# Fetching w1's first piece later and its rest in one transfer, in a kernel of block-sorted attention and routed experts

## The chip, the cores and the metric

The kernel runs on one core of a Trainium2 chip. The core has five engines that work side by side, each with its own queue of instructions: TensorE (PE in the profile, matmuls; PEld its weight loads), VectorE (DVE), ScalarE (ACT), GpSimd (POOL) and SyncE (SP, which here only issues transfers). Sixteen DMA engines move data between the chip's memory and the core's. The metric is the device time of the whole kernel in microseconds (us).

## The reference: what is computed

```python
P = sort_net                                  # 4 x 8 heads, 8 x 8
for _ in range(5):
    P = exp(P - max(P)); P = P / sum(P, rows); P = P / sum(P, columns)
k_sorted = einsum('bhij,bhjcd->bhicd', P, k_blocks)     # 8 blocks of 96 rows
v_sorted = einsum('bhij,bhjcd->bhicd', P, v_blocks)
attn = softmax(scale * q_blocks @ k_sorted.T)           # inside each block
x = (attn @ v_sorted), laid out as 3072 x 512
P = exp(x @ w_gate - max), balanced 8 times over rows and columns
for e in range(8):
    out += P[:, e:e+1] * (maximum(x @ w1[e], 0) @ w2[e])
```

The attention has 4 batches of 8 heads, 768 positions and 64 columns; w1 is 8 x 512 x 1024 and w2 is 8 x 1024 x 512. All inputs are float32 in memory; the kernel works in bfloat16 from the load on.

## The kernel before

The kernel has two stages. In the first, the attention of the four batches is worked out batch by batch, and expert 0 of a batch is computed beside it (lines 97 to 487). In the second (from line 488), experts 1 to 7 follow for all tokens, with seven products of half-size blocks in place of eight. The change lies at the start of the first stage, in the first 30 us.

**Loads.** Whatever has to become bfloat16 on its way is loaded by GpSimd (`load_batch`, `load_rest`, `part_w1`, `load_w2`), and stands in GpSimd's one queue in the order in which it is written. For batch 0 these are the queries, values and keys in halves of four heads (lines 98 and 100), then the first 256 of the 1024 columns of expert 0's w1 (line 108). `part_w1(f0, f1)` (lines 103 to 106) loads such a strip of columns as one transfer: 128 partitions times 4 rows of f1 - f0 columns.

**Sort matrices.** VectorE and ScalarE work out P (lines 426 to 445); TensorE spreads it over the partitions into `pbps` (line 452). `Rt[bb]` is the sorting matrix of a batch, one 128x128 matrix per head. For batch 0 VectorE builds it (line 456); for batch 1 GpSimd does, with the generator `build_r(1, nc.gpsimd, 4)`: two instructions of four heads each (line 133), each followed by a `yield`, so that the caller can put something between them. They read `Pb`, which ScalarE copies at line 464.

**The values' exchange.** `sort_values(0, ...)` multiplies the values by the sort matrices (line 146) and evicts them to `vs` (line 148). The sorted rows then have to move to other partitions: eight transfers of 96 KB, one for each block i (lines 154 to 161), take them from `vs` to `vsb`. For batch 0 their order is 0, 1, 2, 3, 4, 6, 5, 7. Blocks 1 and 3 are issued by ScalarE, 5 and 7 by GpSimd, the others by SP; before block 5 the generator yields, so 5 and 7 are issued only when `values` is resumed at line 467. A transfer that ScalarE or GpSimd issues takes its place among that engine's own instructions.

**The plan.** What TensorE does next is written out by hand in `PLAN0` (line 209), and `pin` keeps each engine's instructions in the order of the program. A letter is a kind of work and its digits are heads and halves: k keys, s scores, d sums, m the mix of scores and values (line 261, the first reader of `vsb`), w warming matmuls whose result nobody reads (line 423), e and h a block of 128 columns of expert 0's hidden layer, l the logits. The steps e00 to e11 (`begin`, line 358) compute hidden blocks 0 and 1, from w1's columns 0 to 255; each h1 (`expert_hidden`, line 368) computes the next block, from 2 (columns 256 to 383) up to 7:

```python
PLAN0 = ("k0 k1 w2 s00 k2 s10 k3 w1 s20 D00 d10 w2 s30 d20 w4 d30 m00 s01 m10 m20 m30 w1 e00 e10 "
         "s11 d01 e01 e11 s21 d11 m01 h1 s31 d21 m11 h1 h1 d31 m21 h1 h1 m31 h1 l0 l3")
```

After the exchange, GpSimd issues the rest of w1 in two pieces (lines 468 and 469), then batch 1's values, half of its keys and queries, expert 0's w2, and the other halves (lines 470 to 472).

Of the kernel before, what the change touches and what calls it, by code (L numbers as in the profile page):

```python
# [20 lines left out]
def mkap(t, dims, off=0):  # L21
    return bass.AP(tensor=t.tensor, offset=t.offset + off, ap=dims)
# [3 lines left out]
def kernel(  # L26
# [11 lines left out]
    nc = tc.nc  # L38
# [33 lines left out]
    def load_batch(bb, parts):  # L72
        for d, name in ((vt, "vt"), (kt, "kt"), (qt, "qt")):
            d[bb] = kvp.tile([128, 8, 384], BF16, name=name, bufs=2)
        load_rest(bb, parts)

    def load_rest(bb, parts):
        for x, l0, n in parts:
            d, src = {"v": (vt, v), "k": (kt, k), "q": (qt, q)}[x]
            pin(nc.gpsimd.dma_start(  # L80
                out=d[bb][:, l0:l0 + n, :],
                in_=src[bb, l0:l0 + n].rearrange("h (p kk) d -> p h (kk d)", kk=6)))
# [9 lines left out]
    def load_w2(e):  # L92
        w2t[e] = (wq if e else wcp).tile([128, 8, Dm], BF16, name="w2e")
        pin(nc.gpsimd.dma_start(out=w2t[e],
                                in_=moe_w2[e].rearrange("(fb k) f -> k fb f", k=128)))
# [7 lines left out]
    def part_w1(f0, f1):  # L103
        pin(nc.gpsimd.dma_start(
            out=w1t[0][:, :, f0:f1],
            in_=moe_w1[0, :, f0:f1].rearrange("(kk k) f -> k kk f", k=128)))

    part_w1(0, 256)
    wg = ones.tile([128, 4, E], BF16)
    pin(nc.gpsimd.tensor_copy(wg, wgf))  # L110
    mask16 = ones.tile([128, 16], F32)
# [17 lines left out]
    def build_r(bb, eng, n):  # L129

        Rt[bb] = perp.tile([128, 8, 8, 16], BF16, name=f"R{bb % 2}")
        for h in range(0, 8, n):
            ins = eng.tensor_tensor(
                out=mkap(Rt[bb], [Rt[bb].ap[0], [16, 8 * n], [1, 16]], off=h * 128),
                in0=mkap(Pb, [Pb.ap[0], [1, 8 * n], [0, 16]], off=(bb * 8 + h) * 8),
                in1=mkap(mask16, [mask16.ap[0], [0, 8 * n], [1, 16]]),
                op=ALU.mult)
            if eng is nc.gpsimd:
                pin(ins)
            yield  # L140


    def sort_values(bb, bank, n=8, h0=0):
        for h in range(h0, n):
            vps = bank([128, 384], F32)
            pin(nc.tensor.matmul(vps, Rt[bb][:, h].rearrange("p i c -> p (i c)"),  # L146
                                 vt[bb][:, h, :], start=True, stop=True))
            (nc.vector.tensor_copy if bb == 0 and h in (3, 5, 7) or bb and h % 2 else
             nc.scalar.copy)(
                vs[:, :, h, :], vps.rearrange("p (kk d) -> p kk d", d=64))  # L150
            if h % 2:
                yield

        for i in (0, 1, 2, 3, 4, 6, 5, 7) if bb == 0 else range(NB if n == 8 else 0):
            eng = ((nc.scalar if i in (1, 3) else nc.gpsimd if i in (5, 7) else nc.sync)
                   if bb == 0 else nc.gpsimd if i % 2 and bb == 1 else nc.sync)
            if bb == 0 and i == 5:
                yield
            (pin if bb == 0 else lambda ins: ins)(eng.dma_start(
                out=mkap(vsbt[bb % 2], [[VW, 96], [1, 512]], off=i * 512),  # L160
                in_=vs[16 * i:16 * i + 16].rearrange("p kk h d -> p kk (h d)")))
# [3 lines left out]
    def queries(bb, hp, bank):  # L165

        qps = bank([128, 6, 128], BF16)
        if bb < 2:

            for kk in range(6):  # L170
                for h in range(2):
                    pin(nc.tensor.matmul(qps[64 * h:64 * h + 64, kk, :],
                                         qt[bb][:, 2 * hp + h, kk * 64:kk * 64 + 64],
                                         Ibig, is_transpose=True, start=True, stop=True))
        else:
            qr = sp.tile([128, 6, 2, 64], BF16, name="qr", bufs=2)
            nc.gpsimd.tensor_copy(
                qr.rearrange("p kk h d -> p h kk d"),
                qt[bb][:, 2 * hp:2 * hp + 2].rearrange("p h (kk d) -> p h kk d", d=64))
            for kk in range(6):  # L180
                pin(nc.tensor.matmul(qps[:, kk, :], qr[:, kk].rearrange("p h d -> p (h d)"),  # L181
                                     Ibig, is_transpose=True, start=True, stop=True))
        qT[bb, hp] = sp.tile([128, 128, 6], BF16, name="qTs", bufs=4)
        (pin if bb == 0 else lambda ins: ins)(
            (nc.scalar.copy if bb == 0 or hp < 2 or bb == 1 else nc.vector.tensor_copy)(
                qT[bb, hp], qps.rearrange("p kk c -> p c kk")))
# [126 lines left out]
    def attention(bb, bank, fill):  # L313

        def sorts():
            for b in {1: (1, 2), 2: (3,), 3: ()}[bb]:
                yield from sort_values(b, bank)
                yield
# [95 lines left out]
    with tc.tile_pool(name="ps0", bufs=7, space=bass.MemoryType.PSUM,  # L414
                      reuse_waits="tile") as ps0, \
            tc.tile_pool(name="psw", bufs=1, space=bass.MemoryType.PSUM) as psw:
        bank0 = lambda shape, dt: ps0.tile(shape, dt, name="bank", tag="bank")
        unread = psw.tile([128, 4, 128], F32)

        def warm(n):  # L420

            for _ in range(n):
                pin(nc.tensor.matmul(unread, Ibig, mkap(Ibig, [Ibig.ap[0], [0, 4], [1, 128]]),
                                     start=True, stop=True))

        pin(nc.vector.reduce_max(out=rs, in_=P, axis=AX.X))
        pin(nc.vector.tensor_sub(P, P, mkap(rs, [rs.ap[0], rs.ap[1], [0, 8]])))
        for it in range(5):
            pin(nc.scalar.activation(out=P, in_=P, func=AF.Exp))
            if it >= 2:  # L430
                queries(0, it - 2, bank0)
            if it == 3:
                warm(4)
            pin(nc.vector.reduce_sum(out=rs, in_=P, axis=AX.X))
            pin(nc.vector.reciprocal(out=rs, in_=rs))
            pin(nc.vector.tensor_mul(P, P, mkap(rs, [rs.ap[0], rs.ap[1], [0, 8]])))
            pin(nc.vector.reduce_sum(out=cs, in_=Pt, axis=AX.X))
            if it == 0:
                pin(nc.vector.tensor_scalar_add(cs, cs, 1e-9))
            pin(nc.vector.reciprocal(out=cs, in_=cs))  # L440
            pin(nc.vector.tensor_mul(Pr.rearrange("p i j -> p j i") if it == 4 else Pt, Pt,
                                     mkap(cs, [cs.ap[0], cs.ap[1], [0, 8]])))
        for eng, i0, n in ((nc.vector.tensor_copy, 0, 5), (nc.scalar.copy, 5, 3)):
            pin(eng(Prep[:, i0:i0 + n],
                    mkap(Pr, [Pr.ap[0], [8, n], [1, 8], [0, 16]], off=i0 * 8)))
        pin(nc.vector.reduce_sum(out=mask16, in_=Ibig.rearrange("p (j c) -> p c j", c=16),
                                 axis=AX.X))
        queries(0, 3, bank0)
        warm(3)
        pbps = bank0([128, 8, 32], F32)  # L450
        for i in range(8):
            pin(nc.tensor.matmul(pbps[:, i, :], Prep[:, i].rearrange("p j c -> p (j c)"),
                                 Ibig[0:32, 0:32], start=True, stop=True))
        Rt[0] = perp.tile([128, 8, 8, 16], BF16, name="R0")
        for h in range(0, 8, 2):
            nc.vector.tensor_tensor(
                out=Rt[0][:, h:h + 2],
                in0=mkap(pbps, [pbps.ap[0], [1, 2], [32, 8], [0, 16]], off=h),
                in1=mkap(mask16, [mask16.ap[0], [0, 2], [0, 8], [1, 16]]), op=ALU.mult)
        warm(2)  # L460
        values = sort_values(0, bank0)
        for _ in range(5):
            next(values)
        nc.scalar.copy(Pb, pbps.rearrange("p i g -> p g i"))
        for _ in build_r(1, nc.gpsimd, 4):
            pass
        next(values, 0)
        part_w1(256, 512)
        part_w1(512, 1024)
        load_batch(1, [("v", 0, 8), ("k", 0, 4), ("q", 0, 4)])  # L470
        load_w2(0)
        load_rest(1, [("k", 4, 4), ("q", 4, 4)])
        def tiles():
            yield from expert_hidden(0, begun["h"], lambda: bank0([128, 512], F32))

        first_attention(bank0, warm, tiles())
# [335 lines left out]
    for m, o in enumerate(ends):  # L812
        e, p, hT, _ = chunks[-1]
# [4 lines left out]
    for r in range(len(pairs) + 6):  # L818
        n, i = r // 4, r % 4
# [84 lines left out]
```

## Time and profile before

| | |
|---|---|
| time, median of 3 runs | 665.8 us (665.04 to 665.95) |
| the profiled execution | 665.01 us, span 663.2 us |
| TensorE busy | 650.9 us, 98% of the span |
| GpSimd busy | 465.9 us, 70% |
| VectorE busy | 475.5 us, 72% |
| ScalarE busy | 386.3 us, 58% |
| TensorE's clock | 0.999 of full speed in the mean |
| transfers issued by GpSimd | 26.81 MB, 25.8% of the 16 DMA engines' time |
| TensorE busy from 0 to 50 us | 41.68 us |
| TensorE busy from 50 to 650 us | 599.8 us |

The span runs from the first to the last instruction of the profiled execution; the device time is a little longer. Every time below counts from the span's start. A group of instructions is named by line, engine, operation and what it writes and reads, with its count, its busy time, the mean duration, and the idle time of the engine just before it with the cause of that. A transfer has two times: when the engine issues it, and how long after that its last byte has landed.

### The profile page before, as it was taken

Reading aid. Unit: us, or ns where it says so; the run is one execution under the profiler, and the core shown is the slowest. Engines: PE = TensorE matmul, PEld = TensorE weight load, DVE = VectorE, ACT = ScalarE, POOL = GpSimd, SP = SyncE. Lnnn points to the kernel's source line nnn. Section 1 sums busy time; section 2 is a strip of 40 time slices with the busy share of each in tenths; the row PEclk is TensorE's granted clock in tenths of the full one; section 3 lists DMA queues with packets and bytes.
Section 4 is the critical chain, followed back from the end, with each engine's and each line's share of the span. In section 5 each row is a group of like instructions: output and inputs, shape, how many; then the busy total and the mean of one; then the engine's idle time right before and its main releaser. Section 6 shows DMA issues by size and latency. Waiting matters only on the chain.

```text
span 663.2 us, 13141 instructions
## 1 busy us (share of the span) xinstructions
PE 650.9 (98%) x5047; PEld 422.3 (64%) x5047; DVE 475.5 (72%) x910; ACT 386.3 (58%) x757; POOL 465.9 (70%) x430
## 2 busy tenths in 40 slices
PE   5999999999999999999999999999999999999997
PEld 2555565555666666666666666666666666666665
DVE  6856576666777777777777777777777777777775
ACT  5777657476777755555555555555555655555540
POOL 3543540196999898779796979698797969846641
PEclk9999999999999999999999999999999999999999
DMA  9999944004303040120303040302103040000224
GB/s 151 177 223 142 195 73 65 1 1 73 55 1 64 1 65 1 27 38 3 61 1 65 1 64 2 65 1 40 26 0 64 1 65 2 1 1 33 96 80 175
DMA packets 33743, 36.52 MB, mean 55 GB/s; under 512 B 2064, under 2 KB 27088, under 8 KB 33680
## 3 DMA queue, kind: packets, MB, share of 16 engines
q0 software_dynamic: 26448, 26.81, 25.8%
q1 hardware_dynamic: 6720, 8.29, 4.4%
q8 instruction: 39, 0.64, 0.4%
q10 hardware_dynamic: 512, 0.59, 0.3%
q14 instruction: 24, 0.20, 0.1%
HBM read 52.45 MB, written 6.29 MB: 89 GB/s over the span
## 4 chain that ended last, share of the span: by engine, by line
PE 96%; DMA 2%; DVE 1%; POOL 1%; issue 0%; ACT 0%; POOLq 0%
PE bk L601 38%; PE oacc L712 38%; PE bank L381 5%; PE bank L368 5%; DMA kt<-in_k_dram 2%; PE bank L220 1%; PE bank L261 1%; PE oacc L784 1%; PE bk L678 1%; PE bank L243 1%; PE bank L196 1%; PE bk L776 1%; PE bank L146 1%; PE oacc L776 1%; PE bk L784 1%; PE bank L181 0%
## 5 line engine op out<-in xcount | busy, mean ns | idle before, releaser
L662 DVE SCALAR_TENSOR_TENSOR osbl<-oacc,glog,osbl 128x256 f32<-128x256 f32 (+1 forms) x411 | 219.4, 535 | 125.6 <-PE oacc L712 116.3
L587 ACT ACTIVATE hT<-bk 128x512 bf16<-128x512 f32 (+1 forms) x176 | 104.2, 592 | 147.5 <-PE bk L601 130.7
L601 PE MATMUL bk<-xtT,w1e 128*128 128x512 bf16 x504 | 149.1, 379 | 0.0
L712 PEld LDWEIGHTS <-hs 128*128 128x128 bf16 x984 | 96.3, 98 | 62.9 <-issue 0.3
L712 PEld LDWEIGHTS <-hT 128*128 128x128 bf16 x904 | 88.4, 98 | 57.9 <-issue 0.6
L702 POOL TENSOR_TENSOR hs<-hT 128x512 bf16<-128x512 bf16 x82 | 95.1, 1159 | 39.8 <-DVE hT L590 34.3
L712 PE MATMUL oacc<-w2e,hT 128*128 128x256 bf16 x764 | 114.6, 273 | 0.2
L702 POOL TENSOR_TENSOR hs<-hs,hT 128x512 bf16<-128x512 bf16 x82 | 94.7, 1154 | 6.4
L601 PE MATMUL bk<-xc,wc 128*128 128x512 bf16 x336 | 99.1, 379 | 0.1
L702 POOL TENSOR_TENSOR hs<-hT,hs 128x512 bf16<-128x512 bf16 x82 | 94.6, 1153 | 6.4
L712 PE MATMUL oacc<-w2e,hs 128*128 128x256 bf16 x616 | 92.4, 273 | 0.0
L601 PEld LDWEIGHTS <-w1e 128*128 128x128 bf16 x672 | 65.8, 98 | 11.6 <-issue 0.3
L590 DVE CUSTOM_DVE_ANT_0 hT<-bk,p 128x512 bf16<-128x512 f32 x84 | 58.1, 691 | 7.7 <-PE bk L601 3.1
L636 ACT COPY p<-bk 128x512 f32<-128x512 f32 x84 | 49.1, 585 | 24.3 <-PE bk L601 23.4
L630 ACT COPY u<-bk 128x512 f32<-128x512 f32 x84 | 49.2, 585 | 22.2 <-PE bk L601 22.1
L621 ACT COPY bk<-bk 128x512 f32<-128x512 f32 x84 | 48.0, 572 | 20.5 <-PE bk L601 20.5
L590 DVE CUSTOM_DVE_ANT_0 hT<-bk,u 128x512 bf16<-128x512 f32 x84 | 57.1, 680 | 1.1 <-PE bk L601 0.6
L712 PE MATMUL oacc<-w2s,hs 128*128 128x256 bf16 x368 | 55.2, 273 | 0.0
L601 PEld LDWEIGHTS <-wc 128*128 128x128 bf16 x504 | 49.3, 98 | 8.0 <-issue 0.2
L655 DVE SCALAR_TENSOR_TENSOR s<-bk,hT 128x512 bf16<-128x512 f32 x80 | 54.4, 680 | 0.0
L601 PE MATMUL bk<-xc,w1e 128*128 128x512 bf16 x168 | 50.0, 379 | 0.0
L601 PE MATMUL bk<-xtT,wc 128*128 128x512 bf16 x168 | 50.0, 379 | 0.0
(140 smaller groups left out, 828.9 us busy)
## 6 DMA issues: line engine op xcount, KB each, us to landing
w2e<-in_moe_w_dram POOLq DMA_DIRECT2D x8, 1024.0 KB, 9.5
w1e<-in_moe_w_dram POOLq DMA_DIRECT2D x7, 1024.0 KB, 8.1
out_dram<-osbl SPq DMA_DIRECT2D x21, 256.0 KB, 2.0
vsb<-vs SPq DMA_DIRECT2D x24, 96.0 KB, 3.1
vt<-in_v_dram POOLq DMA_DIRECT2D x3, 768.0 KB, 11.8
qt<-in_q_dram POOLq DMA_DIRECT2D x4, 384.0 KB, 10.5
kt<-in_k_dram POOLq DMA_DIRECT2D x4, 384.0 KB, 12.2
kt<-in_k_dram POOLq DMA_DIRECT2D x2, 768.0 KB, 15.0
```

The costliest lines, as they stand in the source:

```text
L368: pin(nc.tensor.matmul(hps[:, 0:n], w1t[0][:, kk, fb * 128:(fb + 1) * 128], xtT[:, kk, c0:c0 + n], start=(kk == 0), stop=(kk == 3)))
L381: pin(nc.tensor.matmul(oacc, hTs[:, fb, tt * 128:(tt + 1) * 128], w2t[0][:, fb, :], start=(fb == 0), stop=(fb == 7)))
L587: relu = lambda o, x: nc.scalar.activation(out=o, in_=x, func=AF.Relu)
L590: return nc.vector._custom_dve(TENSOR_ADD_SAT, out=o, in0=x, in1=y, s0=TOP, s1=0.0)
L601: pin(nc.tensor.matmul(ps, wa[:, kk, :], xa[:, kk, :], start=(first and kk == 0), stop=(kk == 1), skip_group_check=True))
L621: pin(nc.scalar.copy(t["w"], t["u"]))
L630: pin(nc.scalar.copy(t["u2"], t["u"]))
L636: pin(nc.scalar.copy(t["p5"], t["v"]))
L655: pin(nc.vector.scalar_tensor_tensor(out=s3[:, i, :], in0=t["w"], scalar=0.0, in1=c12, op0=ALU.max, op1=ALU.subtract))
L662: pin(nc.vector.scalar_tensor_tensor(out=o, in0=ps, scalar=glog[:, t, e:e + 1], in1=o, op0=ALU.mult, op1=ALU.add))
L702: pin(nc.gpsimd.tensor_tensor(out=s[:, c], in0=a, in1=b, op=o))
L712: pin(nc.tensor.matmul(ps, h[:, fb, :], w[:, fb, :], start=(first and fb == 0), stop=(fb == 3), skip_group_check=True))
```

## The change

It has three parts. The load of w1's first 256 columns is taken from its place behind batch 0's loads and is put between the two instructions with which GpSimd builds batch 1's sort matrices. The rest of w1, so far two transfers of 256 and 512 columns, becomes one of 768 columns at the place of the two. And block 3 of batch 0's exchange is issued by SP, not by ScalarE, which keeps block 1.

```diff
@@ -105,7 +105,6 @@
-    part_w1(0, 256)
     wg = ones.tile([128, 4, E], BF16)
     pin(nc.gpsimd.tensor_copy(wg, wgf))
@@ -152,7 +151,7 @@
         for i in (0, 1, 2, 3, 4, 6, 5, 7) if bb == 0 else range(NB if n == 8 else 0):
-            eng = ((nc.scalar if i in (1, 3) else nc.gpsimd if i in (5, 7) else nc.sync)
+            eng = ((nc.scalar if i == 1 else nc.gpsimd if i in (5, 7) else nc.sync)
                    if bb == 0 else nc.gpsimd if i % 2 and bb == 1 else nc.sync)
@@ -462,11 +461,12 @@
         nc.scalar.copy(Pb, pbps.rearrange("p i g -> p g i"))
-        for _ in build_r(1, nc.gpsimd, 4):
-            pass
+        half = build_r(1, nc.gpsimd, 4)
+        next(half)
+        part_w1(0, 256)
+        next(half, 0)
         next(values, 0)
-        part_w1(256, 512)
-        part_w1(512, 1024)
+        part_w1(256, 1024)
         load_batch(1, [("v", 0, 8), ("k", 0, 4), ("q", 0, 4)])
```

## The prediction

> **What bounds the kernel now.** I read the page's first two parts, then the chain of waits from 0 to 80 us, then TensorE's groups in the stretch the change touches, then GpSimd's and ScalarE's timelines there and the DMA issues one by one. TensorE is busy 98% of the span. The chain of waits (start us, length us, what) says where the rest sits:
>
> ```profile
> 5.69 11.89 DMA kt<-in_k_dram
> 17.58 0.04 issue
> 17.62 0.53 PE bank L196 x12
> ...
> 24.01 0.71 PE bank L358 x4
> ...
> 26.66 0.17 PE bank L261 x8
> 26.83 0.76 PE bank L368 x4
> ```
>
> Until 17.58 the chain is the load of the keys; from there it is TensorE without a break, the warming matmuls of L423 included. TensorE's groups between 17.6 and 33 us (busy, mean ns, then idle before and its cause) say the same:
>
> ```profile
> L368 PE MATMUL bank<-xtT,w1e 128*128 128x384 bf16 x24 | 4.6, 328 | 0.0
> L261 PE MATMUL bank<-atp,vsb 96*64 96x96 bf16 x48 | 2.0, 207 | 0.0
> L358 PE MATMUL bank<-xtT,w1e 128*128 128x384 bf16 x8 | 1.7, 326 | 0.0
> L196 PE MATMUL bank<-R,kt 128*64 128x128 bf16 x24 | 1.1, 222 | 0.2 <-DMA kt<-in_k_dram 0.2
> ```
>
> The values' exchange (vsb, read at L261) and all of w1 (L358, L368) arrive in time; only the last keys are 0.2 us late. So nothing of TensorE's can be saved here but that 0.2 us (0.6 with the 0.39 us idle at 15.73, whose cause is ScalarE's eviction of L148), and whatever makes TensorE wait is paid in full, because its order is written out by hand and it is full up to the last microseconds.
>
> GpSimd, whose queue carries every load that casts (start, length):
>
> ```profile
> 6.42 0.79 POOL L104 DMA_DIRECT2D w1e<-in_moe_w_dram  x1
> ...
> 16.47 2.07 POOL L133 TENSOR_TENSOR R<-Pb,mask 128x512 bf16<-128x512 f32 x2 [9.05 <-ACT Pb L464]
> 18.49 1.12 POOL L159 DMA_DIRECT2D vsb<-vs  x2
> 19.58 1.59 POOL L104 DMA_DIRECT2D w1e<-in_moe_w_dram  x2
> 21.13 0.93 POOL L80 DMA_DIRECT2D vt<-in_v_dram  x1
> ```
>
> The DMA issues around 20 us, with the time from issue to landing in the last column, for w1's second and third piece (issued at 19.58 and 20.41):
>
> ```profile
> w1e<-in_moe_w_dram POOLq DMA_DIRECT2D x1, 256.0 KB, 6.6
> w1e<-in_moe_w_dram POOLq DMA_DIRECT2D x1, 512.0 KB, 8.4
> ```
>
> and, from the page, for the whole w1 tiles loaded later on:
>
> ```profile
> w1e<-in_moe_w_dram POOLq DMA_DIRECT2D x7, 1024.0 KB, 8.1
> ```
>
> The reader should set landings against first uses. First piece: 6.42 + 12.5 = 18.9, used at 24.01, 5.1 us to spare. Second: 19.58 + 6.6 = 26.2, used (hidden block 2, columns 256 to 383) at 26.83, 0.6 us to spare. Third: 20.41 + 8.4 = 28.8, used (block 4) after blocks 2 and 3, about 29.0, 0.2 us to spare. These two margins are what the change touches.
>
> **The change, part by part.**
>
> *w1's first piece leaves the early queue.* It was the last of the early loads, behind the keys; its packets (512 B) run from 15.5 to 18.6 us in the trace's packet records, mostly after the keys' own. The keys may land up to 0.2 us earlier (their whole lateness), or not at all.
>
> *It is issued between GpSimd's two sort matrices.* The first matrix ends at 16.47 + 1.05 = 17.52. The issue takes 0.79, so 17.52 to 18.3; the second matrix runs 18.3 to 19.35 (not read before 33.31, L146); the two exchange blocks are issued at 19.35 and 19.9 instead of 18.49 and 19.06; the rest of w1 at about 20.45 to 21.25, and the next batch's values at 21.2 instead of 21.13, since one issue was added ahead and one removed. The exchange blocks 5 and 7 landed 3.7 us after issue, so 23.1 and 23.6, or two more if they queue behind the piece; L261 needs them at 26.49. Covered. The piece itself: exchange block 5, issued by GpSimd at 18.49, had its first packet at 20.1, 1.6 us later, so the piece's packets start near 19.1; 512 rows on 16 engines are 32 rows of 60 ns each, 1.9 us; with the spread between the engines seen at the first queries (2.5 us of packets, 3.8 us from first packet to landing, so 1.3) it lands near 22.3, up to 1 us later beside the other exchange transfers. Needed at 24.01. By the row of the second piece (6.6 us) it would be 24.1. So 0 to 0.3 us of wait, most likely none.
>
> *One exchange block from ScalarE's queue to SP's.* ScalarE's two issues take 16.36 to 17.88, and its first exponential starts at 17.93, though its scores were ready about 17.45:
>
> ```profile
> 16.36 1.52 ACTq L159 DMA_DIRECT2D vsb<-vs  x2
> 17.93 2.21 ACT L234 ACTIVATE atp<-bank 96x384 bf16<-96x384 f32 x5 [1.05 <-DVE kTs L202]
> ```
>
> ScalarE gains up to 0.5 us and TensorE nothing, as it doesn't wait for it. On SP, block 3 takes the third place (17.56), and blocks 4 and 6 slip by 0.6 to 0.9 us. Block 3 lands at 17.56 + 4.1 = 21.7 instead of 17.09 + 4.3 = 21.4; L261 reads it at about 22.5. Blocks 4 and 6 land by 24, read from 26.49. With w1's piece out of the way until 19.1 they should land sooner than that. Cost zero; 0.8 us would have to be lost before TensorE saw it.
>
> *w1's rest in one piece.* This is the term that counts. Hidden block 2 needed a piece of 256 KB; it now needs the last byte of 768 KB. When does that land? Start from the old third piece, 28.8, the moment at which all of w1 was there. Three things move it. (a) The first piece is now in the same stretch of queue ahead of it: 32 rows x 60 ns = +1.9 us. (b) The queue, which had a pause, starts again at 17.52 rather than 18.49: -1.0. (c) One piece has 1536-byte rows instead of 512 and 1024: by the packet records 60, 79, 98 and 172 ns for 512, 768, 1024 and 2048 bytes, so about 136 for 1536, and 32 x (60 + 98) = 5.1 us become 32 x 136 = 4.4: -0.7. Sum +0.2: it lands at 29.0. Block 2 then starts 0.04 later (the keys' landing to L196, above) instead of at 26.83: **29.04 - 26.83 = 2.2 us of wait**. Everything queued behind it on TensorE (the other hidden blocks, the mixes, batch 1) moves by as much. Of what comes after, the next values land at 32.6 and are read at 33.31, now 35.5, and the later loads have the same gain in margin, so no second wait follows. What was gained or lost before block 2, within 2 us, is swallowed by this wait: the keys' 0.2, ScalarE's 0.5, a late first piece.
>
> Bounds of that landing, both from rows. Early: a whole w1 tile with a quiet queue, 8.1 us for 1 MB, of which 32 x 172 ns = 5.5 are its rows; with 4.4 in their place 7.0, so 27.4, a wait of 0.6. Late: the whole tile issued at 64.22 beside an exchange, 10.5 us: 30.9, a wait of 4.1. I take 29.0, nearest to the 8.4 of the piece issued at the same place beside the same neighbours.
>
> On the merging, the row first: the second and third piece landed 2.6 us apart, with 3.1 us of rows in the third, so no fixed cost stood between them that a merge could remove. [...]
>
> **The sum.** 0 (exchange) + 0 (first piece) + 2.2 (rest of w1) with nothing given back. The profiled execution took 665.01 us around a span of 663.2; so 667.2. The three runs have a median of 665.8, 0.8 above it, so **668.0** for a median.
>
> **The rivals.**
>
> 1. *No wait: one transfer beats two and lands before 26.8.* Then all that is left is the keys' 0.2 us, at most 0.6: 665.2 to 665.6, not slower. It decides at 6.4 us from issue to landing. For it: 512 rows instead of 1024, and an exchange that is out of the way earlier. Against: no load of w1 without anything else in the queue was below 8.1 in the median, and the 256 KB piece took 6.6. [...] Chance 7%.
> 2. *A short wait.* The landing is between 26.8 and 28.1, towards the early bound, because the exchange on SP's queue is done sooner: 0.1 to 1.3 us, 665.9 to 667.1. Chance 19%.
> 3. *The wait slows TensorE's clock.* The first four warming matmuls at 7.87, after 6.4 idle us, took 1.89 us; four at 21.13 took 1.04. About 3.4 us after 6.44 ran at half speed, which is 1.7 us lost. If a gap of 2.2 us does the same: 668.0 + 1.7 = 669.7. Against: after the 1.11 us gap before L452 the two warming matmuls at 13.14 took 0.60, full speed; a gap of 2.2 is between the two. [...] Chance 8%.
> 4. *A later landing*, 30 to 31 us, wait 3.2 to 4.2: 669.0 to 670.0. Chance 8%.
>
> My forecast, landing between 28.1 and 30.0, is 667.1 to 669.0, chance 58%. The measurement tells about 0.2% (1.3 us) from no change; so slower 58 + 8 + 8 = 74%, same 23% (rival 2 and most of rival 1), faster 3%, for a saving that no row explains. The range 666.0 to 669.7 leaves out rival 1, a little of rival 2 and the upper part of 3 and 4.
>
> **What would show it.** Right: L368's first matmul at about 29 us with some 2 us of idle time before it, put down to the DMA of w1e; the rest of w1 issued near 20.4 and landing 8 to 9 us later; L358 and L261 without idle time; ScalarE's first exponential near 17.5; warming matmuls of later stretches unchanged. Wrong: L368 without idle time, or idle time before L358 or L261 that is longer than that before L368, or matmuls of 128x384 that take twice their 326 ns after the gap.

## The result, and the profile after

The changed kernel takes 669.79 us (median of 7 runs, 667.52 to 671.56), the kernel before 665.47 us (median of 7, 664.99 to 665.95). The ratio is 1.0062, 95% interval [1.0042, 1.0081]: 4.3 us slower, where 2.2 was forecast, and 0.1 us above the top of the stated range. The profiled execution took 670.72 us (span 668.9), 5.7 more than that of before. From the removed line 108 to the change at line 465, line numbers are one lower than before (L368 is now L367, L261 is L260, L358 is L357).

TensorE's groups between 17.6 and 36 us of the changed kernel:

```profile
L367 PE MATMUL bank<-xtT,w1e 128*128 128x384 bf16 x13 | 3.6, 415 | 3.2 <-DMA w1e<-in_moe_w_dram 3.2
L260 PE MATMUL bank<-atp,vsb 96*64 96x96 bf16 x48 | 2.4, 221 | 0.9 <-DMA vsb<-vs 0.9
L357 PE MATMUL bank<-xtT,w1e 128*128 128x384 bf16 x8 | 1.7, 326 | 0.0
L195 PE MATMUL bank<-R,kt 128*64 128x128 bf16 x24 | 1.1, 223 | 0.2 <-DMA kt<-in_k_dram 0.2
```

Two idle times are new: 0.9 us ahead of the first mix, which waits for an exchange block, and 3.2 us ahead of hidden block 2, which waits for w1. A third sign stands in the mean of L367, 415 ns where it was 328. The keys' 0.2 is still there. GpSimd, and the DMA issues at 17.6 and 20.8 us with their time to landing:

```profile
17.47 0.82 POOL L104 DMA_DIRECT2D w1e<-in_moe_w_dram  x1
18.30 1.07 POOL L132 TENSOR_TENSOR R<-Pb,mask 128x512 bf16<-128x512 f32 x1
19.31 1.11 POOL L158 DMA_DIRECT2D vsb<-vs  x2
20.40 0.82 POOL L104 DMA_DIRECT2D w1e<-in_moe_w_dram  x1
```

```profile
w1e<-in_moe_w_dram POOLq DMA_DIRECT2D x1, 256.0 KB, 7.0
vsb<-vs SPq DMA_DIRECT2D x1, 96.0 KB, 6.0
...
w1e<-in_moe_w_dram POOLq DMA_DIRECT2D x1, 768.0 KB, 10.6
```

The first piece lands at 17.47 + 7.0 = 24.5, block 3 (issued by SP at 17.55) at 23.55, the rest of w1 at 20.40 + 10.6 = 31.0. The chain of waits, from the sort matrices on:

```profile
18.30 1.07 POOL R L132
19.37 1.03 POOL vsb L158 x2
20.40 10.58 DMA w1e<-in_moe_w_dram
31.03 1.46 PE bank L367 x4
```

GpSimd's queue and one transfer now are the chain, and hidden block 2 starts at 31.03 instead of 26.83: 4.2 us. Its four matmuls take 1.46 instead of 0.76. Why, the stages show (length, busy time of PE with its count, and of PEld, DVE, ACT and POOL, then TensorE's granted clock, the DMA engines' share and GB/s):

```profile
27.50:30.90 3.40, 0.37 (x10) 0.20 (x6) 0.90 (x2) 2.06 (x5) 0.00 (x0) 1.00 1.23 187
30.90:34.30 3.40, 3.27 (x24) 1.63 (x25) 0.99 (x2) 1.26 (x4) 0.00 (x0) 0.50 1.32 202
34.30:40.00 5.70, 5.63 (x68) 3.45 (x67) 4.57 (x10) 2.00 (x4) 0.00 (x0) 1.00 1.27 205
```

After the wait TensorE's clock is granted at half for 3.4 us. Batch 1's first values (L145) start at 39.02 instead of 33.31, 5.7 us later: 4.2 of wait and 1.5 of slow clock. The 0.9 us at the exchange are inside the 4.2, not on top: without them TensorE would only have waited longer at block 2.

The clock also orders the runs. The two with a mean of 1.000 took 667.52 and 667.86 us; the four at 0.996 and 0.997 (in the profiled one, 0.997, one half-speed stretch of 3.4 us) 668.76 to 670.72; the one at 0.994 (no profile; by its size two stretches) 671.56.

### The profile page after: what moved, and what is told of

It is laid out like the page before. It is cut to its first block, busy times and chain, and to the rows that moved or that the text cites. A ratio compares the mean times of both kernels' runs of the same rounds, so it can differ in the third digit from the quotient of the medians.

```text
span 668.9 us, 13140 instructions
## 1 busy us (share of the span) xinstructions
PE 652.4 (98%) x5047; PEld 422.8 (63%) x5047; DVE 475.6 (71%) x910; ACT 386.9 (58%) x757; POOL 465.8 (70%) x429
## 4 chain that ended last, share of the span: by engine, by line
PE 94%; DVE 2%; DMA 2%; ACT 1%; POOL 1%; issue 0%
PE bk L601 38%; PE oacc L712 37%; PE bank L380 5%; PE bank L367 5%; DMA w1e<-in_moe_w_dram 2%; PE oacc L784 1%; PE bk L678 1%; PE bank L219 1%; PE bank L260 1%; PE bk L776 1%; PE bank L242 1%; PE bank L195 1%; PE bank L145 1%; PE oacc L776 1%; PE bk L784 1%; PE bank L180 0%
```

## The experiments

The theory after the result: hidden block 2 needs one part in six of the merged transfer but has to wait for its last byte, and a wait of that length costs the clock on top. The rivals: the first piece's later place does it, by pushing everything behind it back; or block 3's place on SP's queue; or the transfer is late because it is one large one. Each time is the median of its runs, beside runs of the kernel before on the same chip.

**The rest of w1 in one piece, alone** (`merge_only`; before with)

```diff
-        part_w1(256, 512)
-        part_w1(512, 1024)
+        part_w1(256, 1024)
```

> The kernel before with w1's rest in one transfer of 768 columns, nothing else: the first piece stays in the early queue and block 3 on ScalarE's queue. Theory 1 (the forecast's: what counts is when the last byte of w1 lands, and merging by itself makes that earlier): the rest lands about 0.7 us sooner than the old third piece, at 28.1, and TensorE waits 1.3 us before hidden block 2 at full clock: 666.8 us, +1.3. Rival (the rows of the merged piece are slow beside what shares the queue, whoever is ahead of it): it lands near 31 as in the changed kernel, a wait of 3 to 4 us and half the clock for 3.4 us: +4 to +6 us. Rival that the first piece's place alone is what costs: no wait, 665.5.

Measured: 669.4 us against 665.54, ratio 1.0053 [1.0041, 1.0066]: +3.9. The rest lands at 19.74 + 9.8 = 29.5, and the group of block 2 shows

```profile
L368 PE MATMUL bank<-xtT,w1e 128*128 128x384 bf16 x20 | 5.7, 445 | 3.0 <-DMA w1e<-in_moe_w_dram 3.0
```

This one edit brings 3.9 of the 4.3 us. Theory 1 as I had sized it (28.1, +1.3) is wrong: merging did not make the end of w1 earlier, but 0.6 us later (GpSimd ran 0.16 late in this execution; 29.4 against 28.8). The rival had the kind of loss right, a wait and then half the clock, but put the landing near 31, 1.5 us too late. The stages (columns as above) show two half-speed stretches, 28.5 to 35.3 us, worth 2.7 of this execution's 5.4:

```profile
25.10:28.50 3.40, 1.52 (x23) 0.83 (x22) 1.58 (x3) 3.17 (x8) 0.25 (x1) 1.00 1.13 166
28.50:31.90 3.40, 2.31 (x18) 1.13 (x20) 0.56 (x1) 0.33 (x1) 0.00 (x0) 0.50 1.28 195
31.90:35.30 3.40, 3.40 (x22) 1.50 (x20) 1.39 (x3) 1.44 (x4) 0.00 (x0) 0.50 1.31 201
```

**The first piece late, alone** (`first_late_only`; before with)

```diff
-    part_w1(0, 256)
...
-        for _ in build_r(1, nc.gpsimd, 4):
-            pass
+        half = build_r(1, nc.gpsimd, 4)
+        next(half)
+        part_w1(0, 256)
+        next(half, 0)
```

> The kernel before with w1's first piece issued between the two sort matrices, the rest in two pieces as before, block 3 on ScalarE's queue. Theory 1: the second piece lands about 1 us later than before (27.1 instead of 26.2) and the third at 29.7 instead of 28.8: waits of 0.3 us before block 2 and some 0.6 before block 4, +0.9 us, 666.4, clock at full. Rival (the piece's packets and the exchange's hold each other up, so the exchange and the whole queue behind it slip by 2 us): block 3 lands above 22.5 with idle time before L261, the second piece near 28.5, the third near 31: +2 to +3 us.

Measured: 666.07 against 665.54, 1.0011 [1.0002, 1.0019]: +0.5. The two pieces land where theory 1 had them, 20.40 + 6.7 = 27.1 and 21.2 + 8.5 = 29.7, each 0.9 later than before. In the profiled execution neither is waited for, because TensorE had lost 1 us earlier (0.57 more than before at keys that came late, 0.45 behind ScalarE's exponentials, which stood behind its two issues). Block 3, which ScalarE issued here at 17.60, after the piece, landed at 23.55, as late as from SP in the changed kernel; it too was not waited for only because TensorE was late. The piece's place does not carry the loss.

**Block 3 on SP's queue, alone** (`block3_only`)

```diff
-            eng = ((nc.scalar if i in (1, 3) else nc.gpsimd if i in (5, 7) else nc.sync)
+            eng = ((nc.scalar if i == 1 else nc.gpsimd if i in (5, 7) else nc.sync)
```

> The kernel before with block 3 of the exchange issued by SP, nothing else. Theory 1: block 3 is issued at 17.56 and lands near 21.7, no idle time before L261, 665.5 us, within 0.1 us of before. Rival (SP's queue is what made block 3 land at 23.55 in the changed kernel): it lands above 22.5, L261 waits 0.3 to 1 us, and with no later wait to swallow it the time is 665.8 to 666.5.

Measured: 665.65 against 665.54, 1.0001 [0.9992, 1.001]: no difference. No idle time before L261; block 3 landed 4.4 us after its issue at 17.6, so 22.0.

**The wait filled with work** (`after_filled`; after with `w9 w3` ahead of the first h1)

```diff
-             "s11 d01 e01 e11 s21 d11 m01 h1 s31 d21 m11 h1 h1 d31 m21 h1 h1 m31 h1 l0 l3")
+             "s11 d01 e01 e11 s21 d11 m01 w9 w3 h1 s31 d21 m11 h1 h1 d31 m21 h1 h1 m31 h1 l0 l3")
```

> The changed kernel with 12 warming matmuls (128x512, unread) in TensorE's order between the mix m01 and hidden block 2, where it waits for w1's rest: 12 x 0.243 = 2.9 us of work inside the wait of 3.2. Theory that a part of the loss is the halved clock after the wait (1.5 of the 5.7 us of the profiled execution): the clock stays at full, every run lies between 669.0 and 669.7, and the spread of the changed kernel (667.5 to 671.6) shrinks to below 1 us. Rival (the spread comes from the landing, the clock costs nothing that shows): the runs still reach 671 or more.

Measured: 668.88 (668.28 to 668.98) against 665.54, 1.0045 [1.0033, 1.0057], clock 1.000 in all five runs. Twelve matmuls that do nothing kept the clock at full in these runs and brought the spread from 4 us to 0.7: the clock is part of the loss. The median is 0.9 us below the changed kernel's, which is not clear of the scatter of these few runs. The filling also has a price: it takes 2.8 us even where the load lands sooner, and no filled run is as fast as the changed kernel's two at full clock (667.52 and 667.86).

**The change with two pieces** (`after_two_pieces`; after with the two old lines for the rest)

> The changed kernel with w1's rest in two pieces again (256 and 512 columns); the first piece late and block 3 on SP's queue as changed. Theory 1 (the loss hangs on hidden block 2 needing the last byte of the merged piece): the second piece lands near 27.2, the third near 29.8; block 3 lands near 23.5 and holds L260 up by 0.9 us, which now nothing swallows; no wait before block 2: 666.3 to 666.6, +0.9, clock at full. Rival (the first piece's later place makes the whole queue late and merging adds little): 668 or more.

Measured: 666.55 against 665.45, 1.0014 [1.0006, 1.0023]: +1.1, with one of eleven runs at a clock of 0.997. TensorE's groups between 27 and 34 us, and the wait that is left, from the groups between 15 and 40:

```profile
L367 PE MATMUL bank<-xtT,w1e 128*128 128x384 bf16 x24 | 4.6, 328 | 0.0
```

```profile
L260 PE MATMUL bank<-atp,vsb 96*64 96x96 bf16 x48 | 2.2, 208 | 1.1 <-DMA vsb<-vs 1.1
```

As theory 1 said: the exchange block's lateness, swallowed before, is now the whole loss, and undoing the merge takes back 3.2 us.

**The change with block 3 on ScalarE again** (`after_block3_back`)

> The changed kernel with block 3 issued by ScalarE again; the first piece late and the rest merged as changed. Theory 1 (whatever is lost before block 2 is swallowed by its wait): the idle time before L260 may shrink from 0.9 to 0, the rest lands between 30.3 and 31, and the time is that of the changed kernel, 669 to 670, with the same spread and clock. Rival (block 3's place on SP's queue sets back the loads behind it): the rest lands at 29.5 and the time falls to 668.5 or less.

Measured: 671.23 (667.63 to 672.07) against 665.45, 1.0075 [1.0057, 1.0093]. The idle time before L260 is gone (block 3, issued 0.4 us earlier, lands near 21.5), the rest lands at 20.45 + 10.3 = 30.75, and the time does not fall. Whatever was gained before block 2 was lost in front of it. That 671.23 lies above 669.79 can't be told from the spread. The clock was expected to be that of the changed kernel, and was not: five of the six runs have 0.994 or 0.995, against one of seven there. In the profiled one it was at half from 28.9 to 35.7 us, two stretches. Whether block 3's place or chance makes the difference stays open.

**Two transfers, but both needed** (`rest_by_rows`; before with)

```diff
-    def part_w1(f0, f1):
+    def part_w1(f0, f1, k0=0, k1=4):
         pin(nc.gpsimd.dma_start(
-            out=w1t[0][:, :, f0:f1],
-            in_=moe_w1[0, :, f0:f1].rearrange("(kk k) f -> k kk f", k=128)))
+            out=w1t[0][:, k0:k1, f0:f1],
+            in_=moe_w1[0, 128 * k0:128 * k1, f0:f1].rearrange("(kk k) f -> k kk f", k=128)))
...
-        part_w1(256, 512)
-        part_w1(512, 1024)
+        part_w1(256, 1024, 0, 2)
+        part_w1(256, 1024, 2, 4)
```

> The kernel before with w1's rest again in two transfers, but split by w1's rows: 384 KB with rows 0 to 255, 384 KB with rows 256 to 511, both over columns 256 to 1023. Hidden block 2 sums over all rows, so it needs both. Theory 1 (what counts is which bytes block 2 needs, not the number of transfers): the second lands near 29.4, TensorE waits 2.5 to 3 us before the third matmul of block 2, and the time is 668 to 670, as with one transfer. Rival (a transfer of 768 KB is late because of its size): both have landed by 28.1, a wait of at most 1.3 us: 666.0 to 666.8.

Measured: 669.66 against 665.45, 1.0056 [1.0038, 1.0074]: +4.2. TensorE does two matmuls of block 2 and stops for the other half:

```profile
27.20 0.50 PE L368 MATMUL bank<-xtT,w1e 128*128 128x384 bf16 x2 [0.39 <-DMA w1e<-in_moe_w_dram]
30.30 0.82 PE L368 MATMUL bank<-xtT,w1e 128*128 128x384 bf16 x2 [2.61 <-DMA w1e<-in_moe_w_dram]
```

As many transfers as before and the same loss as with one, although the second landed at 30.3, 0.9 us later than expected. What counted here was how many bytes stood between the consumer and the last one it needed.

**The rest cut after block 2's columns** (`after_128_first`; after with)

```diff
-        part_w1(256, 1024)
+        part_w1(256, 384)
+        part_w1(384, 1024)
```

> The changed kernel with the rest of w1 in two pieces cut elsewhere: columns 256 to 383 (what hidden block 2 alone needs), then 384 to 1023. If each hidden block waits for the last byte of its own transfer and for nothing else, block 2 starts without a wait near 28, and block 3 waits for the second piece, which lands near 30.7, from about 29.6 on: a wait of 1 to 1.5 us, on top of the 1.1 that the two-piece kernel lost: 667.5 to 668.3. If a later, larger piece holds up the smaller one ahead of it, block 2 waits as well: 669 or more.

Measured: 666.88 against 665.5, 1.0019 [1.0011, 1.0027]: +1.4. Block 2 starts without a wait, hidden blocks 3 and 4 (one row below) wait 0.86 us for the 640 KB:

```profile
27.25 0.82 PE L367 MATMUL bank<-xtT,w1e 128*128 128x384 bf16 x4
29.70 1.48 PE L367 MATMUL bank<-xtT,w1e 128*128 128x384 bf16 x8 [0.86 <-DMA w1e<-in_moe_w_dram]
```

These land at 29.7, 1 us sooner than expected, and the time is below the expected 667.5. The dependence is as the theory has it; the landing was mis-sized again.

**Half the filling** (`after_fill6`; after with `w6` ahead of the first h1)

> The changed kernel with 6 warming matmuls (1.46 us) ahead of hidden block 2, which leaves some 1.7 us of the wait idle. In the two profiles with a wait the clock fell after stretches of 3.4 us in which TensorE had been busy for 0.4 and 1.5 us. Theory (a stretch must be less than about half busy): 1.7 us idle leaves every stretch at half or more, the clock stays at full, and all runs lie at 668.2 to 669.2. Rival (a gap above 1.1 us is enough): some runs show a clock of 0.997 or less and 670 or more.

Measured: 669.05 (667.47 to 671.42) against 665.45, 1.0044 [1.0031, 1.0057]; two of six runs at a clock of 0.997. The theory's range does not hold, and the rival's sign is there (671.42 us at 0.997), but it does not decide: in just that execution, the profiled one, the rest landed at 31.6, so 2.9 us stayed idle, not 1.7, and neither theory had been asked about that.

**The wait by itself** (`gap1`, `gap2`, `gap3`; before, with n GpSimd additions that TensorE waits for, all loads untouched, `g1`, `g2` or `g3` ahead of the first h1)

```diff
+    def gap(n):
+        g = mps.tile([128, 384], BF16, name="gap", bufs=1)
+        for j in range(n):
+            pin(nc.gpsimd.tensor_tensor(out=g, in0=begun["h"][:, 1] if j == 0 else g,
+                                        in1=begun["h"][:, 0], op=ALU.add))
+        pin(nc.tensor.matmul(unread_[0][:, 0:128], g[:, 0:128], Ibig, start=True, stop=True))
```

> The kernel before with a wait of known length put where the changed kernel waits: ahead of hidden block 2 one GpSimd addition (128x384, about 0.9 us), which starts when hidden block 1 is written, and one small unread matmul that waits for it. All loads stay as before. So TensorE idles about 0.9 us with no transfer in the play. If the clock falls only after a stretch of 3.4 us that TensorE spent less than about two thirds busy (59% fell, 79% did not in the profiles so far), it never falls here: 666.4 to 666.6, clock at full in every run.

> The same with two additions: some 1.8 us of idle time. Full clock throughout gives 667.3. If a stretch of 3.4 us that is under two thirds busy is enough, the clock falls in those executions whose stretches hold most of the gap, and not in those that the gap straddles: a part of the runs at a clock of 0.997 and 668.5 to 669, the others at 667.3. If it takes a whole idle stretch, all runs are at 667.3 and full clock.

> The same with three additions: some 2.6 us. Full clock gives 668.1. If under two thirds busy is enough, nearly all runs lose the clock for 3.4 or 6.8 us and lie at 669.5 to 671. If it takes a whole idle stretch of 3.4 us, all are at 668.1 and full clock.

Measured, against 665.5 (a run that lost the clock is one whose mean clock is 0.997 or less):

| | idle time | time | ratio | runs that lost the clock |
|---|---|---|---|---|
| gap1 | 1.0 us | 666.25 | 1.0005 [0.9992, 1.0019] | 0 of 11 |
| gap2 | 2.0 us | 667.33 | 1.0033 [1.002, 1.0047] | 4 of 9 |
| gap3 | 3.0 us | 670.74 | 1.0071 [1.0059, 1.0084] | 5 of 5 |

With two additions the runs fall in two groups, 666.83 to 667.33 at a clock of 1.000 and 668.52 to 669.97 at 0.997 or 0.994, 1.2 us apart at the nearest. With three, every run loses one stretch or two. (Without any added wait the kernel before lost a stretch in 2 of the 26 runs beside these.) The stages of gap3 show both sides of the fall, with no load in the play (the clock column is 0.96 and 0.54 where the clock changed a little inside the stage):

```profile
25.80:29.20 3.40, 0.78 (x19) 0.54 (x18) 1.31 (x3) 2.43 (x6) 2.52 (x4) 0.96 1.25 194
29.20:32.60 3.40, 3.03 (x24) 1.59 (x25) 0.64 (x2) 0.94 (x3) 0.32 (x1) 0.50 1.32 202
32.60:36.00 3.40, 3.40 (x20) 1.57 (x19) 1.61 (x4) 1.22 (x3) 0.00 (x0) 0.54 1.30 205
```

By the trace's clock records the clock was at half from 28.93 to 35.76, two stretches. TensorE was busy 1.06 us of the 3.41 before that, and 2.77 of the first slow stretch.

## Why the prediction was right, and where not

**What bounds the kernel: right.** TensorE had nothing to gain in this stretch, and what it waited for was paid in full.

**The first piece: its place right, its landing 2 us off.** It was issued at 17.47 and landed at 24.5, not near 22.3; the row of the second piece (24.1) was the better measure. It was used at 24.89, only because the exchange had already made TensorE late. In `after_block3_back`, where that was not so, L357 idled 0.5 us and started at 24.59, just after the piece's landing at 24.51; the profile names VectorE's xtT for that idle time, but the piece for the weight load that goes with it.

**The exchange: wrong, but without effect on the sum.** ScalarE's first exponential starts at 17.47, as said, and gains nothing. But block 3 landed 2 us later than forecast and TensorE waited 0.9 us for it. The step that failed is "cost zero", since I took 4.1 us to landing from a profile without w1's piece beside it. Alone, block 3 on SP costs nothing (`block3_only`); issued after the first piece it landed at 23.0 to 23.8 in six profiles, in one of them from ScalarE's queue (`first_late_only`), and issued by ScalarE at 17.15, before the piece, at 21.5 (`after_block3_back`). So it is the piece ahead of it, not SP's queue, that makes it late, and once block 2's wait no longer covers it, it costs about 1 us (`after_two_pieces`). Blocks 4 and 6 landed at 24.2 and 25.1, not by 24 or sooner, which cost nothing.

**The rest in one piece: the mechanism right, the size not.** Block 2 did wait for the last byte. Term by term: (a) and (b), the first piece ahead and the earlier start, were put at +0.9, and `first_late_only` measured +0.9 on both pieces. (c), the merge, was put at -0.7, and `merge_only` measured +0.6. In the trace's packet records the 1536-byte rows took 135 ns in the median, as interpolated (136), but 155 in the mean in the changed kernel and 174 in `merge_only`, because 54 and 69 of the 512 took over 200. The two pieces they replace took 71 and 106 ns a row in the mean in the kernel before (60 and 98 in the median), 5.7 us together against 5.0 and 5.6. So (c) compared undisturbed rows, and in `merge_only` there was next to nothing to save. Nor does the lateness sit in most of the rows: nine tenths had started by 27.3 us in the third piece before and by 27.4 in `merge_only`, the last at 28.3 and 29.1. 28.8 + 0.9 + 0.6 gives 30.3; the profile has 31.0, and the last 0.7 stays unexplained. The four profiles with the first piece late and the rest in one transfer land at 30.7 to 31.6, all above 30.3, so the two effects seem to do more together than their sum; no run shows why.

**The bounds** of the landing, 27.4 and 30.9, just failed to hold the 31.0.

**The later landing, rival 4 at 8%, came true** in the profiled execution: it landed at 31.0, and block 2 started 4.2 us later, the upper end that the rival gave. Rivals 3 and 4 together, 665.0 + 4.2 + 1.5, make the 670.7 of that execution; the prediction priced each by itself and never the two at once. That the median lies as near to the range as 0.1 us is in part luck: without the two runs that kept their clock it would be 670.3. Of the prediction's own signs of being wrong one showed, the matmuls of 128x384 at half speed after the gap, and of its signs of being right one did not, since the first mix had idle time before it.

**The clock: the rival that I gave 8% came true** in five of seven runs, the profiled one among them. I had set a harmless gap of 1.1 us against a harmful one of 6.4 and called 2.2 "between the two"; `gap1` to `gap3` now say where, in this place: 1.0 us of idle time kept the clock in all 11 runs, 2.0 us lost it in 4 of 9, 3.0 us in 5 of 5. The price, 1.7 us estimated, was 1.5 in the profiled execution and 2.7 where two stretches ran slow (`merge_only`). The half speed after 6.44 us, from which the 1.7 was worked out, lasted about 4.0 us in the profile of before, to 10.4, not 3.4: of the 24 matmuls of L172 that start at 9.87, those before 10.2 take 314 to 316 ns, as at 6.44 (314), and those from 10.5 on 218 or 219; that would make it 2.0. Had the wait been 2.2 us as forecast, this rival would, by `gap2`, still have been close to even. The two runs at full clock, +2.1 and +2.4 us, lie on the forecast of 2.2; since they have no profile, that the rest landed near 29.0 in them is an inference.

The half-speed stretches lasted 3.41 us in the changed kernel (30.92 to 34.34 in its clock records) and twice that, 6.83, in `gap3`. A whole idle stretch of 3.4 us, the alternative that `gap2` and `gap3` set against the theory, was not needed: the idle time at which the clock fell was 3.16 us in the changed kernel, 2.97 in `merge_only`, 3.27 in `after_block3_back`, 2.99 in `gap3` and 2.01 in `gap2`. In the 3.4 us before the fall TensorE had been busy for 0.36 us (changed kernel), 1.5 (`merge_only`) and 2.0 (`after_block3_back`); in `gap1`, where the clock stayed, for 2.38 of the 3.40 us from 25.8 to 29.2. Why some executions of `gap2` kept the clock and others lost it, no run shows.

**Not slower (rival 1): refuted** by `merge_only`. One transfer did not beat two here: the rival needed a landing before 26.8, and the rest landed at 29.5 in `merge_only` and at 31.0 in the changed kernel.

No experiment came out faster than the kernel before; `block3_only` equals it.

## What to carry to other kernels

Cut a load where its consumers are cut. In `merge_only` hidden block 2 started at 29.59 us, with the landing of all 768 KB (29.5), though it reads a sixth of them; so merging two loads made the first consumer wait for the bytes of the second, and whether a merge gains anything in rate has to be set against that. When a queue of loads feeds an engine that is full, compare each piece's landing with its first use before merging or reordering; here the margins were 0.6 and 0.2 us. And a wait of TensorE can cost more than its length: here 3.0 us of idle time cost 5.2 (`gap3`), and 2.0 us lost the clock in 4 of 9 runs (`gap2`). Unread matmuls put into it kept the clock here; what that gains in the median was not clear of the scatter.

## What the runs showed of the hardware that was not expected

A wait shorter than the 3.41 us of a half-speed stretch was enough to lose the clock: 2.0 us of idle time in 4 of 9 runs, 3.0 in 5 of 5. After a half-speed stretch that was only partly busy the clock stayed at half: in `merge_only` TensorE was busy 2.31 of the 3.4 us from 28.5 to 31.9, in `gap3` 2.77 of 3.41, and both times the next 3.4 us ran at half speed too; after the changed kernel's stretch with 3.3 us of work the clock was full.

The end of the merged transfer was late out of proportion. Of its 512 packets in the changed kernel, nine tenths had started by 28.05 us and the last at 30.36; for a consumer that needs all of it, the last tenth cost 2.3 us. In the four other profiles whose rest of w1 is one transfer it was 1.0 to 2.4 us. Which DMA engines make that tail the records do not tell, and it was not tried.
